# Phase 2 of a fused attention and two-stage MLP kernel: a bank for each product of the last groups, w_out blocks merged in the first half, a fixed order in the second

## The chip, the cores and the metric

The kernel runs on one core of a Trainium2 chip. The metric is the device time of one execution in microseconds; the time before is the median of three runs. A profiled execution of the same kernel gives the rows below.

## The reference

```
attn = softmax(scale * q k^T + slope * bias, causal window of 128) v      # 4 x 8 heads, 576 tokens, 64 wide
x = attn as 2304 tokens x 512
y = ((x w1) * (x w2)) w3 w_out_1          # 512 -> 1024 -> 512
h = max(y w_in, 0)                        # 512 -> 2048
out = (h * h) w_out                       # 2048 -> 512
```

All weights are float64 (the draws of NumPy are not cast), the activations and the output float32.

## The kernel before

Phase 1 (to 458.8 us of the span) makes y, transposed, in DRAM (y_scr). Phase 2 does the last two lines of the reference, and it alone is changed.

Every float32 product is made of three matmuls, since an operand is split into a high part (rounded by a copy, on ACT or DVE) and a low part (the difference, on DVE or POOL): high x high, high x low, low x high (mm3s, L1130 to 1133). A product that reads a high part can start before the low part is there, until its third matmul.

Both halves of phase 2 use Winograd's form of Strassen: a 2 x 2 block product is seven products P1 to P7 and some sums. Sums of inputs are made ahead (combine, L856; comb in add_o, L1275); sums of outputs behind: with U2 = P1 + P6 and U4 = U2 + P5 the blocks are C11 = P1 + P2, C12 = U4 + P3, C21 = U2 + P7 + P4, C22 = U4 + P7, up to signs that lie in the inputs.

*First half (add_r, L1209):* 24 groups (r, j, m) for three blocks j of 768 tokens and eight pairs m of columns of w_in. A product is six matmuls of 384 columns. The results get a relu and go to DRAM (s_scr, L1228). *Second half (add_o, L1243):* nine groups (o, t) of 256 tokens; a product is 24 matmuls of 256 columns over all eight blocks of w_out. Its inputs come back from s_scr (L1253), are squared on ACT (L1261), combined on DVE (L1275), and split into high (L200) and low parts (L203), tiles ww, st or u.

A group (add_group, L1147) has three PSUM banks, tags xa, xb and xc with two buffers each. xa gathers P1, P6, P5, P3, and between them it is copied out: C11 starts as P1 (task c1), C21 as U2 (u2), C22 as U4 (u4); so P6 waits for c1, P5 for u2 and P3 for u4. P7 and P4 gather in xb, P2 in xc; adds on DVE (L1192) finish the blocks. Tasks copy by L200 or L1183 (relu) on ACT and L260 on DVE.

Weights come as float64, two words per element. A block is merged to float32 words by three instructions: ACT scales the high words (L330), DVE shifts the low ones (L339) and ORs both (L345). w_in's blocks and blocks 5 to 7 of w_out are merged in phase 1 and kept in DRAM (add_merge, L870, m_scr); blocks 0 to 4 of w_out are loaded and merged in the last third of the first half (add_words2, L879). Then each block gets four sums (L868), a high and a low copy of the four plain parts (tile u) and of the three sums (tile v).

Every task (products, copies, adds, DMAs) has a rank, dependences, tiles to take and to give back, and a planner (Plan.run) writes all of them out in one order by its own costs; each engine's queue then holds its tasks in that order and runs them one behind the other, SP's DMAs as well. In add_group the order within a group is free but for the dependences, and P4 depends on P7 in all cases. A group called with last (the last of the first half, and (o, 0)) has a second xc bank (tag xd) for P4.

Of the kernel before, what the change touches and what calls it, by code (L numbers as in the profile page):

```python
# [152 lines left out]
def fused_kernel(  # L153
# [56 lines left out]
    NM = NF2 // 2  # L210
    s_scr = [dram.tile([NF2, 128, 2 * TN], F32, name=f"s_scr{j}") for j in range(NJ)]
    m_scr = {(k, m): dram.tile([128, 1024], F32, name=f"m_scr{k}{m}") for k in "ic" for m in range(NM)}
    m_scr.update({("o", m): dram.tile([128, 1024], F32, name=f"m_scro{m}") for m in range(OM, NM)})


    ident = const.tile([128, 128], F32, name="ident")
# [579 lines left out]
    A_AT = {1: "a0", 2: "a1", 3: "b2", 4: "a3", 5: "b0", 6: "b1", 7: "a2"}  # L796
    B_AT = {1: "a0", 2: "a2", 3: "a3", 4: "b2", 5: "b0", 6: "b1", 7: "a1"}
    PO = (1, 2, 6, 7, 5, 3, 4)
    ORDER = ((1, 2, 4, 6, 7, 5, 3), PO)
    lastp = [None]  # L800
    pool = {}
    late = ExitStack()
# [344 lines left out]
    def add_group(g, n, prod, fin, rank, last=False):  # L1147
        z = "".join(str(x) for x in g)
        w = 24 * w_mm(256) if g[0] == "o" else 6 * w_mm(TN)
        for nm, tag in (("xa", "xa"), ("xb", "xb"), ("xc", "xc"), ("C11", "D1"), ("C21", "D2"), ("C22", "D4"), ("C12", "D3")):  # L1150
            hold(nm + z, tag, 1)
        steps = [
            (1, "xa", [], True), (2, "xc", [], True), (6, "xa", ["c1"], False), (7, "xb", [], True),
            (5, "xa", ["u2"], False), (3, "xa", ["u4"], False), (4, "xb", ["c22"], False),
        ]
        if last:
            hold("xd" + z, "xc", 1)
            p4 = (4, "xd", [], True)
            steps = [*steps[:2], steps[3], p4, steps[2], *steps[4:6]] if g[0] == "r" else [*steps[:2], p4, *steps[2:6]]
        for i, (P, nm, dep, first) in enumerate(steps):  # L1160
            deps, gives, fn = prod(P)
            deps = deps + [d + z for d in dep] + {6: [f"P1{z}"], 5: [f"P6{z}"], 3: [f"P5{z}"], 4: [f"P7{z}"]}.get(P, [])
            if P == 1 and lastp[0]:
                deps = deps + lastp
            if P == 1:
                lastp[0] = f"P1{z}"

            def go(e, P=P, nm=nm, first=first, fn=fn, **kw):
                if first and not kw.get("c0"):
                    bank[g, nm] = new("xc" if nm == "xd" else nm, [128, 512])[:, 0:n]  # L1170
                fn(bank[g, nm], first, **kw)

            if g == ("o", 0) and P in (1, 2):
                add(f"Q{P}{z}", rank + i, {"pe": 0.75 * w}, lambda e, go=go: go(e, c0=0, c1=6),
                    [d for d in deps if d[-2:] not in ("o6", "o7")], [nm + z])
                add(f"P{P}{z}", rank + i, {"pe": 0.25 * w}, lambda e, go=go: go(e, c0=6, c1=NM), deps + [f"Q{P}{z}"], [], gives)
            else:
                add(f"P{P}{z}", rank + i, {"pe": w}, go, deps, [nm + z] if first else [], gives)
# [19 lines left out]
        if last:  # L1198
            plus("d21", "21", "xb", ["u2", "P7", "c22"], ["xb"], -20)
            plus("c21", "21", "xd", ["d21", "P4"], ["xd"], -20)  # L1200
        else:
            plus("c21", "21", "xb", ["u2", "P4", "c22"], ["xb"], -20)
        if g[0] == "r":
            add("c12" + z, -20, w_act(n), lambda e: cp(e, "12", "D3", ACTF.Relu), [f"P3{z}"], [f"C12{z}"], [f"xa{z}"])
        else:
            add("c12" + z, -20, w_copy(n, True), lambda e: cp(e, "12", "D3"), [f"P3{z}"], [f"C12{z}"], [f"xa{z}"])
        fin(z)

    def add_r(j, m, rank, last):  # L1209
# [8 lines left out]
        def fin(z):  # L1218
            def relu(e, c):
                x = cs[g, c]  # L1220
                if e == "a":
                    nc.scalar.activation(out=x, in_=x, func=ACTF.Relu)  # L1222
                else:
                    nc.vector.tensor_scalar(out=x, in0=x, scalar1=0.0, scalar2=None, op0=ALU.max)

            def st(c):
                i, h = int(c[0]) - 1, int(c[1]) - 1
                nc.sync.dma_start(out=s_scr[j][m + NM * i, :, TN * h:TN * h + TN], in_=cs.pop((g, c)))  # L1228

            for c in ("11", "12", "21", "22"):  # L1230
                if c != "12":
                    add(f"sq{c}{z}", rank + 16, w_act(TN), lambda e, c=c: relu(e, c), [f"c{c}{z}"])
                add(f"ss{c}{z}", -15, {"dma": w_dma(197)}, lambda e, c=c: st(c), [f"sq{c}{z}" if c != "12" else f"c12{z}"], [], [f"C{c}{z}"])

        add_group(g, TN, prod, fin, rank, last)


    ow = {}
    fa = {}
    FT = {"A11": "fo", "A21": "fo", "A12": "fq", "A22": "fq", "S1": "fq", "S2": "fq"}  # L1240
    A_OF = {1: "A11", 2: "A12", 3: "S2", 4: "A22", 5: "S1", 6: "S2", 7: "A21"}

    def add_o(t, rank, last):  # L1243
        j, t0 = divmod(256 * t, 2 * TN)
# [38 lines left out]
        order = ORDER[t > 0]  # L1283
        chain = {}
        for tag_ in (True, False):
            seq = [P for P in order if (P in (1, 2)) == tag_]
            before = [P for P in ORDER[t > 1] if (P in (1, 2)) == tag_][-1]
            for x, P in enumerate(seq):
                chain[P] = [f"oh{seq[x - 1]}{t}"] if x else [f"oh{before}{t - 1}"] if t else []
        for pos, P in enumerate(order):  # L1290
# [30 lines left out]
            for c in ("11", "12", "21", "22"):  # L1321
                add(f"ss{c}{z}", -15, {"dma": w_dma(131)}, lambda e, c=c: st(c), [f"c{c}{z}"], [], [f"C{c}{z}"])

        add_group(g, 256, prod, fin, rank, t == 0)


    load_order = [("w3", 0), ("wo", 0), ("w3", 1), ("wo", 1), ("wo", 2), ("w3", 2), ("wo", 3)] + [("w3", i) for i in range(3, 8)]
# [145 lines left out]
```

## Time and profile before

| | |
|---|---|
| median of three runs | 826.41 us (826.1 to 827.46) |
| the profiled execution's own time | 828.39 us |
| its span, first to last instruction | 826.6 us |
| mean granted clock of TensorE | 0.998 of full |
| busy: PE, DVE, ACT, POOL | 807.8, 612.3, 467.4, 60.3 us |
| phase 2, first half | 458.8 to 639.6 us |
| phase 2, second half | 639.6 us to the end |

PE is TensorE's matmuls, DVE is VectorE, ACT ScalarE, POOL GpSimd, SP the engine that issues DMAs. Matmuls overlap: each row of one lasts longer than the step to the next, so a busy PE is not PE at its peak, and steps from start to start tell its pace. A row's idle time ends with what released it. Rows with one line number (L200, L203) are those of helpers; their tiles tell them apart.

### The profile page before, as it was taken

To read this page: it belongs to the slowest core of one execution; us is meant where nothing else is said; L and a number is where in the kernel's file an instruction comes from. 1 tells how busy PE (TensorE), PEld (TensorE's weight loads), DVE (VectorE), ACT (ScalarE), POOL (GpSimd) and SP (SyncE) were. 2 spreads that over 40 slices of the span, in tenths; PEclk is the share of its full clock that TensorE was granted. 3 is DMA by queue.
4 is the path that set the end of the run, shared out by engine and by line. 5 is a ranking of instruction groups with operands and counts; after the bars stand their busy time and mean duration, and the time that the engine had idled before them with its cause. 6 is when DMAs were issued, how large, how long until landed. Compare 5 with 4: busy or idle time off the path is not lost.

```text
span 826.6 us, 17260 instructions
## 1 busy us (share of the span) xinstructions
PE 807.8 (98%) x6732; PEld 750.2 (91%) x6732; DVE 612.3 (74%) x1359; ACT 467.4 (57%) x1007; POOL 60.3 (7%) x68
## 2 busy tenths in 40 slices
PE   8899999999999999999999999999999899999998
PEld 7666556699999899999999999999998899999998
DVE  6898888966798997897498565523697887676762
ACT  7898978633333442342244576645688766666531
POOL 1000000000001000210040220000114010000000
PEclk9999999999999999999999999999999999999999
DMA  9989897798623542112231553522894755444200
GB/s 228 288 257 282 272 280 248 273 328 273 213 83 118 192 174 85 63 33 73 63 127 64 182 179 125 193 104 102 288 300 149 210 156 152 133 143 135 87 27 33
DMA packets 96961, 138.75 MB, mean 168 GB/s; under 512 B 10864, under 2 KB 74864, under 8 KB 94832
## 3 DMA queue, kind: packets, MB, share of 16 engines
q1 hardware_dynamic: 96880, 137.65, 53.2%
q8 instruction: 53, 0.87, 0.5%
q14 instruction: 28, 0.23, 0.1%
HBM read 95.81 MB, written 41.81 MB: 167 GB/s over the span
## 4 chain that ended last, share of the span: by engine, by line
PE 89%; DVE 6%; ACT 2%; DMA 1%; issue 1%; POOL 0%; SPq 0%; DVEq 0%; POOLq 0%; ACTq 0%
PE xa L1131 8%; PE xa L1133 8%; PE xa L1132 8%; PE g L659 6%; PE g L195 6%; PE g L196 6%; PE g L197 6%; PE xb L1131 4%; PE xb L1133 4%; PE xb L1132 4%; PE s L467 3%; PE al L1080 3%; PE al L1082 3%; PE al L1081 3%; PE t L503 2%; PE xc L1131 2%
## 5 line engine op out<-in xcount | busy, mean ns | idle before, releaser
L1192 DVE TENSOR_TENSOR D<-xb,D 128x384 f32<-128x384 f32 (+1 forms) x66 | 34.0, 518 | 59.8 <-PE xb L1133 30.8
L196 PE MATMUL g<-gt,wu 128*128 128x288 f32 x256 | 75.7, 296 | 0.0
L195 PE MATMUL g<-gt,wu 128*128 128x288 f32 x256 | 75.6, 295 | 0.0
L197 PE MATMUL g<-gt,wu 128*128 128x288 f32 x256 | 75.4, 295 | 0.0
L200 ACT ACTIVATE D<-xa 128x384 f32<-128x384 f32 (+1 forms) x100 | 45.2, 454 | 40.9 <-PE xa L1133 38.8
L443 ACT ACTIVATE e<-e,st 128x192 f32<-128x192 f32 (+1 forms) x144 | 62.2, 435 | 9.1 <-DVE st L435 8.8
L659 PE MATMUL g<-raw 128*128 128x512 f32 x128 | 62.5, 603 | 0.2
L203 DVE TENSOR_TENSOR ww<-fq,ww 128x1024 fp32r<-128x1024 f32 x34 | 41.6, 1222 | 24.2 <-ACT ww L200 23.8
L1080 PE MATMUL al<-x,wc 128*128 128x288 f32 x192 | 57.5, 299 | 1.1 <-ACT d L200 1.1
L1082 PE MATMUL al<-x,wc 128*128 128x288 f32 x192 | 56.7, 295 | 0.0
L200 ACT ACTIVATE ww<-fq 128x1024 fp32r<-128x1024 f32 x35 | 37.0, 1057 | 34.8 <-PE xa L1133 18.6
L1081 PE MATMUL al<-x,wc 128*128 128x288 f32 x192 | 56.6, 295 | 0.0
L200 ACT ACTIVATE ye<-g 128x288 f32<-128x288 f32 x32 | 13.1, 410 | 73.5 <-PE g L197 68.0
L1222 ACT ACTIVATE D<-D 128x384 f32<-128x384 f32 x72 | 37.2, 521 | 24.3 <-DVE D L1192 24.2
L196 PEld LDWEIGHTS g<-gt,wu 128*128 128x128 f32 x256 | 48.3, 189 | 0.0
L197 PEld LDWEIGHTS g<-gt,wu 128*128 128x128 f32 x256 | 48.2, 188 | 0.0
L195 PEld LDWEIGHTS g<-gt,wu 128*128 128x128 f32 x256 | 48.1, 188 | 0.0
L868 DVE TENSOR_TENSOR st<-st 128x256 f32<-128x256 f32 (+1 forms) x103 | 40.7, 428 | 9.1 <-DMA st<-m_scrc 5.5
L200 ACT ACTIVATE d<-al 128x288 f32<-128x288 f32 x71 | 28.7, 409 | 32.2 <-PE al L1082 23.6
L503 PEld LDWEIGHTS t<-ident,e 128*128 128x128 f32 x208 | 23.7, 140 | 22.6 <-ACT pt L200 9.9
L435 DVE CUSTOM_DVE_ANT_0 e<-s,bw 128x192 f32<-128x192 f32 (+1 forms) x128 | 40.6, 351 | 3.3 <-PE s L467 3.1
L467 PE MATMUL s<-qk 64*64 64x128 f32 (+2 forms) x768 | 38.2, 287 | 4.6 <-issue 1.9
(269 smaller groups left out, 2787.5 us busy)
## 6 DMA issues: line engine op xcount, KB each, us to landing
s_scr<-D SPq DMA_DIRECT2D x96, 192.0 KB, 1.9
u<-in_w2io_dram SPq DMA_DIRECT2D x22, 512.0 KB, 7.5
fo<-s_scr SPq DMA_DIRECT2D x20, 512.0 KB, 4.6
qk<-in_qk_dram SPq DMA_DIRECT2D x32, 288.0 KB, 5.9
st<-m_scrc SPq DMA_DIRECT2D x18, 512.0 KB, 3.8
raw<-in_w3t_dram SPq DMA_DIRECT2D x8, 1024.0 KB, 8.1
raw<-in_w_dram SPq DMA_DIRECT2D x8, 1024.0 KB, 8.3
fq<-s_scr SPq DMA_DIRECT2D x16, 512.0 KB, 4.8
```

The lines of the kernel that those rows point to most:

```text
L195: nc.tensor.matmul(o, wh, xh, start=start, stop=False)
L196: nc.tensor.matmul(o, wh, xl, start=False, stop=False)
L197: nc.tensor.matmul(o, wl, xh, start=False, stop=stop)
L200: nc.scalar.activation(out=o, in_=i, func=ACTF.Copy)
L467: nc.tensor.matmul(HD[2 * m + r]["s"][g][o, c:c + w], t[h, 0, 64 * q:64 * q + 64], t[h, 1, 64 * k:64 * k + w], start=True, stop=True,)
L659: nc.tensor.matmul(gw[fi], wl, wr, start=c == 0, stop=c == 7)
L1080: nc.tensor.matmul(o, wh, xh, start=start and c == 0, stop=False, skip_group_check=True)
L1081: nc.tensor.matmul(o, wh, xl, start=False, stop=False, skip_group_check=True)
L1082: nc.tensor.matmul(o, wl, xh, start=False, stop=c == 1, skip_group_check=True)
L1131: nc.tensor.matmul(o, wh, xh, start=start, stop=False, skip_group_check=True)
L1132: nc.tensor.matmul(o, wh, xl, start=False, stop=False, skip_group_check=True)
L1133: nc.tensor.matmul(o, wl, xh, start=False, stop=stop, skip_group_check=True)
```

## The change

1. A new add_last takes the place of add_group for the last group of each half, (r, 2, 7) and (o, 8). Every product has a bank of its own: P1 and P5 in xa, P6 and P3 in xb, P2 and P4 in xc, P7 in a bank of the older pool g. The products stand in the order 1, 6, 5, 3, 2, 7, 4. Only P1 is copied; u2, u4, c12, c11, d21, c22 and c21 are adds on DVE of a bank and an SBUF block. In (r, 2, 7) C12 then gets its relu by an instruction of its own.
2. Blocks 0 to 4 of w_out are merged by add_merge too, in the first half of phase 2, one after the other in the one free buffer of tag u, behind the last weights of w_in; the words are stored in m_scr and loaded back when add_words2 needs them.
3. In (o, 0) P4 no longer depends on P7. The turns of the second half's products are written out as a list, each depending on the one before, and ORDER has a row for every t.

```diff
-    m_scr.update({("o", m): dram.tile([128, 1024], F32, name=f"m_scro{m}") for m in range(OM, NM)})
+    m_scr.update({("o", m): dram.tile([128, 1024], F32, name=f"m_scro{m}") for m in (*range(OM, NM), *range(OM))})
...
-    ORDER = ((1, 2, 4, 6, 7, 5, 3), PO)
+    ORDER = ((1, 2, 4, 6, 7, 5, 3), *[PO] * (NT // 256 - 2), (1, 6, 5, 3, 2, 7, 4))
...
     def add_group(g, n, prod, fin, rank):
...
-        if last:
+        first_o = g == ("o", 0)
+        if first_o:
             hold("xd" + z, "xc", 1)
-            p4 = (4, "xd", [], True)
-            steps = [*steps[:2], steps[3], p4, steps[2], *steps[4:6]] if g[0] == "r" else [*steps[:2], p4, *steps[2:6]]
+            steps = [*steps[:2], (4, "xd", [], True), *steps[2:6]]
...
-            deps = deps + [d + z for d in dep] + {6: [f"P1{z}"], 5: [f"P6{z}"], 3: [f"P5{z}"], 4: [f"P7{z}"]}.get(P, [])
+            deps = deps + [d + z for d in dep] + {6: [f"P1{z}"], 5: [f"P6{z}"], 3: [f"P5{z}"], 4: [] if nm == "xd" else [f"P7{z}"]}.get(P, [])
...
+    def add_last(g, n, prod, fin, rank):
+        z = "".join(str(x) for x in g)
+        for nm, tag in (("C11", "D1"), ("C21", "D2"), ("C22", "D4"), ("C12", "D3")):
+            hold(nm + z, tag, 1)
+        use = {1: 1, 6: 1, 5: 1, 3: 1, 2: 1, 7: 2, 4: 1}
+        for i, (P, tag) in enumerate(((1, "xa"), (6, "xb"), (5, "xa"), (3, "xb"), (2, "xc"), (7, "g"), (4, "xc"))):
+            deps, gives, fn = prod(P)
+            hold(f"B{P}{z}", tag, use[P])
...
+            def go(e, P=P, tag=tag, fn=fn):
+                bank[g, P] = (ps_g.tile([128, 512], F32, tag="g", name="g") if tag == "g" else new(tag, [128, 512]))[:, 0:n]
+                fn(bank[g, P], True)
+            add(f"P{P}{z}", rank + 0.1 * i, {"pe": 6 * w_mm(TN) if g[0] == "r" else 24 * w_mm(256)}, go, deps, [f"B{P}{z}"], gives)
...
+        add("c1" + z, -30, w_copy(n, True), one, [f"P1{z}"], [f"C11{z}"], [f"B1{z}"])
...
+                nc.vector.tensor_tensor(out=cs[g, o], in0=bank[g, P], in1=cs[g, b], op=ALU.add)
...
+        plus("u2", 6, "11", "21", "D2", ["c1"], -30)
+        plus("u4", 5, "21", "22", "D4", ["u2"], -30)
+        plus("c12", 3, "22", "12", "D3", ["u4"], -20)
+        plus("c11", 2, "11", "11", None, ["c1", "u2"], -20)
+        plus("d21", 7, "21", "21", None, ["u4"], -20)
+        plus("c22", 7, "22", "22", None, ["c12"], -20)
+        plus("c21", 4, "21", "21", None, ["d21"], -20)
+        fin(z)
...
-        add_group(g, TN, prod, fin, rank, last)
+        (add_last if last else add_group)(g, TN, prod, fin, rank)
...
-        add_group(g, 256, prod, fin, rank, t == 0)
+        (add_last if last else add_group)(g, 256, prod, fin, rank)
...
+        if (k, m) == ("o", 0):
+            prev = ["wlbi7"]
         add_merge(k, m, RANK["mg"] + RANK["mgs"] * x, prev)
...
-        prev = [f"{'mb' if m >= OM else 'ld'}o{m}"]
+        prev = [f"mbo{m}"]
+    turn = ["Q1o0", "P1o0", "Q2o0", "P2o0", "P4o0", "P6o0", "P7o0", "P5o0"]
+    for t in range(1, NT // 256):
+        turn += [f"P1o{t}", f"P3o{t - 1}", *([f"P4o{t - 1}"] if t > 1 else []), *(f"P{P}o{t}" for P in ((2, 6, 7, 5) if t < NT // 256 - 1 else (6, 5, 3, 2, 7, 4)))]
+    for x, y in zip(turn, turn[1:]):
+        turns[y] = [x]
     for t in range(NT // 256):
-        add_o(t, r, False)
+        add_o(t, r, t == NT // 256 - 1)
```

(Q1 and Q2 of (o, 0) are the first three quarters of P1 and P2, which need blocks 0 to 5 only.)

DVE's queue at the seam of the two halves, before: the end of group (r, 2, 7) and the inputs of (o, 0). The tiles u and v behind st are low parts of weights, u and ww behind fo and fq low parts of inputs of the second half, D the blocks of a group, fq<-fo and fq<-fq,fo the combinations.

```order
L203 TENSOR_TENSOR u<-st,u 128x1024
L1192 TENSOR_TENSOR D_7584<-xb,D_7584 128x384
L203 TENSOR_TENSOR v_7639<-st,v_7639 128x768
L260 COPY D_7666<-xa 128x384
L1192 TENSOR_TENSOR D_7666<-xb,D_7666 128x384
L1192 TENSOR_TENSOR D_7652<-xb,D_7652 128x384
L1192 TENSOR_TENSOR D_7652<-xc,D_7652 128x384
L203 TENSOR_TENSOR u<-fo,u 128x1024
L203 TENSOR_TENSOR v_7680<-st,v_7680 128x768
L1275 TENSOR_TENSOR fq<-fo 128x1024
L1275 TENSOR_TENSOR fq<-fq,fo 128x1024
L203 TENSOR_TENSOR ww<-fo,ww 128x1024
```

The same place after (L1238 is the add of add_last, L1319 the combinations):

```order
L1238 TENSOR_TENSOR D_7657<-xb,D_7622 128x384
L203 TENSOR_TENSOR u<-st,u 128x1024
L1238 TENSOR_TENSOR D_7669<-xa,D_7657 128x384
L203 TENSOR_TENSOR st<-fo,st 128x1024
L1238 TENSOR_TENSOR D_7622<-xc,D_7622 128x384
L1238 TENSOR_TENSOR D_7689<-xb,D_7669 128x384
L1238 TENSOR_TENSOR D_7669<-g,D_7669 128x384
L1238 TENSOR_TENSOR D_7657<-g,D_7657 128x384
L1238 TENSOR_TENSOR D_7657<-xc,D_7657 128x384
L1319 TENSOR_TENSOR fq<-fo 128x1024
L203 TENSOR_TENSOR u<-fo,u 128x1024
L1319 TENSOR_TENSOR fq<-fq,fo 128x1024
```

The low part of P1's input (st<-fo) is now on DVE, ahead of the group's last five adds; before it was on POOL. The low part of block 7's sums (v<-st) has left this row for POOL. P2's low part (u<-fo) stood ahead of the first combination (fq<-fo) and stands behind it now.

SP's queue in the first half after the change, around the store of block 2 (m_scro) and the load for block 3 (u<-in_w2io_dram, two halves); s_scr<-D are stores of the groups' results. Before, only rows of the kind s_scr<-D stood here.

```order
L1270 DMA s_scr_93<-D_6619 128x384
L849 DMA m_scro_116<-u 128x1024
L1270 DMA s_scr_93<-D_6713 128x384
L1270 DMA s_scr_93<-D_6723 128x384
L1270 DMA s_scr_93<-D_6742 128x384
L1270 DMA s_scr_93<-D_6695 128x384
L843 DMA u<-in_w2io_dram 128x1024 x2
```

The load for block 3 stands behind the last store of group (r, 1, 2) (D_6695); it reuses the buffer that the store of block 2 reads.

ACT's queue after the change, around the scaling of block 3 (L330):

```order
L1264 ACTIVATE D_6762<-D_6762 128x384
L1264 ACTIVATE D_6790<-D_6790 128x384
L200 ACTIVATE D_6828<-xa 128x384
L330 ACTIVATE u<-u 128x1024
L200 ACTIVATE D_6846<-xa 128x384
L200 ACTIVATE D_6855<-xa 128x384
```

The scaling stands between two copies out of bank xa: behind that of U2 of group (r, 1, 4) (D_6828) and ahead of that of U4 (D_6846), for which P3 of the group waits. The other four stand in like places.

## Rows read from the trace of the kernel before

**Rows 1.** The page, busy time, share of the span and instructions of each engine.

```profile
PE 807.8 (98%) x6732; PEld 750.2 (91%) x6732; DVE 612.3 (74%) x1359; ACT 467.4 (57%) x1007; POOL 60.3 (7%) x68
```

**Rows 2.** Table of stretches: length, busy PE, PEld, DVE, ACT, POOL, clock, DMA, GB/s.

```profile
458.76:574.15 115.39, 115.39 (x656) 115.39 (x655) 56.83 (x99) 69.23 (x141) 12.63 (x13) 1.00 0.45 155
574.15:639.58 65.43, 63.85 (x355) 62.19 (x355) 51.60 (x82) 52.56 (x91) 15.39 (x13) 1.00 0.73 236
639.58:661.02 21.44, 19.08 (x145) 18.66 (x145) 18.28 (x18) 15.97 (x19) 0.65 (x1) 0.92 0.73 206
661.02:814.06 153.04, 153.04 (x1298) 153.04 (x1297) 110.26 (x115) 87.69 (x105) 2.96 (x1) 1.00 0.40 114
814.06:823.60 9.54, 8.95 (x74) 8.54 (x72) 0.50 (x2) 0.77 (x2) 0.00 (x0) 1.00 0.09 29
```

**Rows 3.** Timeline of TensorE: start, length, instruction, idle before it and releaser.

```profile
632.38 0.44 PE L1131 MATMUL xa<-yA,v 128*128 128x384 f32 x1 [0.26 <-ACT D L200]
...
636.46 0.44 PE L1131 MATMUL xa<-yA,v 128*128 128x384 f32 x1 [0.63 <-ACT D L200]
...
638.43 0.44 PE L1131 MATMUL xa<-yA,v 128*128 128x384 f32 x1 [0.65 <-DVE D L260]
...
640.28 0.39 PE L1133 MATMUL xa<-u,st 128*128 128x256 f32 x1 [0.29 <-POOL st L203]
...
648.37 0.39 PE L1133 MATMUL xa<-u,ww 128*128 128x256 f32 x1 [2.07 <-DVE ww L203]
...
817.52 0.39 PE L1131 MATMUL xa<-u,ww 128*128 128x256 f32 x1 [0.47 <-ACT D L200]
```

**Rows 4.** Table of stretches, the one behind the wait at 648.37; columns as in rows 2.

```profile
648.37:652.70 4.33, 4.33 (x23) 4.33 (x24) 3.35 (x3) 2.50 (x3) 0.00 (x0) 0.61 0.98 281
```

**Rows 5.** Timeline of DVE around the seam: start, length, instruction.

```profile
629.16 1.76 DVE L203 TENSOR_TENSOR u<-st,u 128x1024 fp32r<-128x1024 f32 x1
630.85 0.55 DVE L1192 TENSOR_TENSOR D<-xc,D 128x384 f32<-128x384 f32 x1
...
642.10 1.21 DVE L1275 TENSOR_TENSOR fq<-fo 128x1024 f32<-128x1024 f32 x1
643.35 1.22 DVE L1275 TENSOR_TENSOR fq<-fq,fo 128x1024 f32<-128x1024 f32 x1
644.49 1.22 DVE L203 TENSOR_TENSOR ww<-fo,ww 128x1024 fp32r<-128x1024 f32 x1
645.63 1.22 DVE L1275 TENSOR_TENSOR fo<-fo 128x1024 f32<-128x1024 f32 x1
```

**Rows 6.** The page, costliest groups: the relu of a block on ACT.

```profile
L1222 ACT ACTIVATE D<-D 128x384 f32<-128x384 f32 x72 | 37.2, 521 | 24.3 <-DVE D L1192 24.2
```

**Rows 7.** Timeline of DVE, the last instruction of the program's last chain.

```profile
823.52 0.42 DVE L1192 TENSOR_TENSOR D<-xb,D 128x256 f32<-128x256 f32 x1 [5.60 <-PE xb L1133]
```

**Rows 8.** Timeline of DVE, the shift and the OR of a block's merge.

```profile
607.41 0.68 DVE L339 TENSOR_SCALAR st<-st 128x1024 uint32<-128x1024 uint32 x1
...
608.94 1.21 DVE L345 SCALAR_TENSOR_TENSOR st<-st 128x1024 uint32<-128x1024 uint32 x1
```

**Rows 9.** Table of stretches of 20 us; columns as in rows 2.

```profile
500.00:520.00 20.00, 20.00 (x115) 20.00 (x114) 11.12 (x21) 12.96 (x30) 0.73 (x1) 1.00 0.35 118
540.00:560.00 20.00, 20.00 (x115) 20.00 (x114) 4.46 (x8) 9.06 (x19) 0.00 (x0) 1.00 0.33 118
600.00:620.00 20.00, 20.00 (x115) 20.00 (x115) 19.74 (x34) 17.26 (x30) 3.22 (x3) 1.00 0.96 297
```

**Rows 10.** Timeline of POOL near the seam: start, length, instruction, idle before.

```profile
627.60 3.92 POOL L868 TENSOR_TENSOR st<-st 128x256 f32<-128x256 f32 x3 [1.92 <-DMA st<-m_scro]
```

**Rows 11.** A late load: SP's issue, ACT's scaling; and the issues of 603 to 607 us.

```profile
581.63 0.85 SPq L843 DMA_DIRECT2D st<-in_w2io_dram  x2
...
589.68 1.18 ACT L330 ACTIVATE st<-st 128x1024 f32<-128x1024 f32 x1 [0.87 <-DMA st<-in_w2io_dram]
...
st<-in_w2io_dram SPq DMA_DIRECT2D x2, 512.0 KB, 5.7
```

More of the change, by code (lines that the diff above doesn't have):

```diff
@@ L1145, in p_o, with add_group @@
             mm3s(o, a[:, 0, 128 * c:128 * c + 128], a[:, 1, 128 * c:128 * c + 128], bh, bl, start and c == 0, c == NM - 1)
[L1147 removed]
+    def add_group(g, n, prod, fin, rank):
         z = "".join(str(x) for x in g)
@@ L1171, in go @@
                 fn(bank[g, nm], first, **kw)
-            if g == ("o", 0) and P in (1, 2):
+            if first_o and P in (1, 2):
                 add(f"Q{P}{z}", rank + i, {"pe": 0.75 * w}, lambda e, go=go: go(e, c0=0, c1=6),
-                    [d for d in deps if d[-2:] not in ("o6", "o7")], [nm + z])
+                    [d for d in deps if d[-2:] not in ("o6", "o7")] + turns.get(f"Q{P}{z}", []), [nm + z])
                 add(f"P{P}{z}", rank + i, {"pe": 0.25 * w}, lambda e, go=go: go(e, c0=6, c1=NM), deps + [f"Q{P}{z}"], [], gives)
             else:
-                add(f"P{P}{z}", rank + i, {"pe": w}, go, deps, [nm + z] if first else [], gives)
+                add(f"P{P}{z}", rank + i, {"pe": w}, go, deps + turns.get(f"P{P}{z}", []), [nm + z] if first else [], gives)
         def cp(e, c, tag, func=None):
@@ L1197, in add_group @@
         plus("c11", "11", "xc", ["c1", "P2"], ["xc"], -20)
-        if last:
+        if first_o:
             plus("d21", "21", "xb", ["u2", "P7", "c22"], ["xb"], -20)
@@ L1206, in add_group, with one, plus, fn @@
             add("c12" + z, -20, w_copy(n, True), lambda e: cp(e, "12", "D3"), [f"P3{z}"], [f"C12{z}"], [f"xa{z}"])
+        fin(z)
[7 more added lines that the diff above has]
+            hold(f"B{P}{z}", tag, use[P])
+            if P == 1:
+                deps = deps + lastp
+                lastp[0] = f"P1{z}"
+            deps = deps + turns.get(f"P{P}{z}", [])
+            def go(e, P=P, tag=tag, fn=fn):
+                bank[g, P] = (ps_g.tile([128, 512], F32, tag="g", name="g") if tag == "g" else new(tag, [128, 512]))[:, 0:n]
+                fn(bank[g, P], True)
+            add(f"P{P}{z}", rank + 0.1 * i, {"pe": 6 * w_mm(TN) if g[0] == "r" else 24 * w_mm(256)}, go, deps, [f"B{P}{z}"], gives)
+        def one(e):
+            t = cs[g, "11"] = new("D1", [128, TN])[:, 0:n]
+            copy(e, t, bank[g, 1])
+        add("c1" + z, -30, w_copy(n, True), one, [f"P1{z}"], [f"C11{z}"], [f"B1{z}"])
+        def plus(nm, P, b, o, tag, deps, rank):
+            def fn(e):
+                if tag:
+                    cs[g, o] = new(tag, [128, TN])[:, 0:n]
+                nc.vector.tensor_tensor(out=cs[g, o], in0=bank[g, P], in1=cs[g, b], op=ALU.add)
+            add(nm + z, rank, w_tt(n, "d"), fn, [f"P{P}{z}"] + [d + z for d in deps], [f"C{o}{z}"] if tag else [], [f"B{P}{z}"])
+        plus("u2", 6, "11", "21", "D2", ["c1"], -30)
[5 more added lines that the diff above has]
+        plus("c21", 4, "21", "21", None, ["d21"], -20)
         fin(z)
@@ L1230, in fin @@
             for c in ("11", "12", "21", "22"):
-                if c != "12":
+                if c != "12" or last:
                     add(f"sq{c}{z}", rank + 16, w_act(TN), lambda e, c=c: relu(e, c), [f"c{c}{z}"])
-                add(f"ss{c}{z}", -15, {"dma": w_dma(197)}, lambda e, c=c: st(c), [f"sq{c}{z}" if c != "12" else f"c12{z}"], [], [f"C{c}{z}"])
-        add_group(g, TN, prod, fin, rank, last)
+                add(f"ss{c}{z}", -15, {"dma": w_dma(197)}, lambda e, c=c: st(c), [f"sq{c}{z}" if c != "12" or last else f"c12{z}"], [], [f"C{c}{z}"])
+        (add_last if last else add_group)(g, TN, prod, fin, rank)
     ow = {}
@@ L1241, in fused_kernel @@
     A_OF = {1: "A11", 2: "A12", 3: "S2", 4: "A22", 5: "S1", 6: "S2", 7: "A21"}
+    turns = {}
     def add_o(t, rank, last):
@@ L1282, in add_o @@
         src = {1: f"fsA11{t}", 6: f"fc1{t}", 2: f"fsA12{t}", 7: f"fc2{t}", 5: f"fc0{t}", 3: f"fc3{t}", 4: f"fsA22{t}"}
-        order = ORDER[t > 0]
+        order = ORDER[t]
         chain = {}
@@ L1286, in add_o @@
             seq = [P for P in order if (P in (1, 2)) == tag_]
-            before = [P for P in ORDER[t > 1] if (P in (1, 2)) == tag_][-1]
+            before = [P for P in ORDER[t - 1] if (P in (1, 2)) == tag_][-1]
             for x, P in enumerate(seq):
```

## The prediction, made before the changed kernel ran

> **What bounds the kernel now.** I read the page's busy times first: TensorE is busy 98% of the span [rows 1], so only what TensorE waits, or runs slowly, can be won. Next, the table of stretches, cut where phase 2 changes its work [rows 2]. In the first stretch TensorE does 109 products of six matmuls, 654 in all (two more reach in from the phase before), in 115.39 us: 0.1764 us each, with no wait. At that pace the 354 matmuls of the second stretch (the last 59 products of the first half) need 62.46 us and take 65.43: **2.97 lost**. In the fourth stretch 54 products of 24 matmuls, 1,296 in all, take 153.04 us: 0.1181 each, no wait. So the third stretch (six products, 144 matmuls) needs 17.00 us and takes 21.44: **4.44 lost**. In the last stretch P5 to P3 of the last group should start 24 x 0.1181 = 2.83 us apart; P3 starts at 817.52 [rows 3] instead of 816.90, and its restart adds about 0.1: **0.75 lost**. All of phase 2 has 8.16 us that a gapless order would not have.
>
> Then the timeline of TensorE, to see what each wait was for [rows 3]. Its idle figure understates the loss, since a matmul's row lasts longer than its step (0.34 against 0.18, 0.28 against 0.12): add 0.16 to each. Three waits for copies out of bank xa (P3 of group (2,6), P5 and P3 of (2,7)) cost 0.42, 0.79 and 0.81, with 0.1 for each restart 2.3 of the 2.97; some 0.65 is left in small pieces. At 640.28 the first product of the second half waits for a low part made on POOL: 0.45. At 648.37 P6 of group (o,0) waits 2.07 for its low part on DVE: 2.23. And behind that wait the granted clock is 0.61 on average over 4.33 us [rows 4], that is, mostly the lower of its two levels: 23 matmuls that need 2.72 us take 4.34, 1.6 more. Last, 817.52 waits for a copy: 0.63.
>
> **The change, part by part.** *Own banks in the last group of each half.* P6, P5 and P3 no longer add onto P1's bank, so TensorE waits for no copy there. That removes the waits of 0.79 and 0.81 at (2,7), with restarts 1.8, and the 0.75 in (o,8). What it adds: u2, u4 and c12 become adds on DVE, about 0.55 each [rows 5], and one relu on ACT, 0.52 [rows 6]. At (o,8) nothing waits for these but the end: there the last chain is one add of a bank and a store, as now [rows 7], so the tail costs what it did. At (2,7) five adds in a row stand on DVE between the low part of P1(o,0) and the combination S1; that is priced below.
>
> *The w_out blocks 0 to 4 merged earlier.* Per block two loads, a scaling on ACT (1.18 us), a shift and an OR on DVE (0.7 and 1.2) [rows 8] move from the stretch 580 to 612 to some 495 to 570. DVE had 19.74 of 20 us busy at 600 to 620, but 11.1 and 4.5 of 20 in the two quieter stretches [rows 9]; 9.5 us of DVE work and 5.8 of ACT fit there. The DMA share was 0.96 in the late stretch, and 0.33 to 0.35 in the others; five stores and five loads back of 0.5 MB each are added, and 5 MB of loads are moved, so the late stretch gets lighter by half of what it loaded. Weights are then ready earlier, DVE is not behind at the seam, P3 of (2,6) no longer waits (0.52 with its restart) and POOL no longer makes the first low part (0.55). Of the small pieces, 0.65, I take 0.2 as left (bounds 0 and 0.65).
>
> *P4 of (o,0) before P6, fixed turns.* P4's wait for P7 was needless with a bank of its own. It now gives TensorE 2.83 us while DVE makes the low part for P6. From the fourth stretch on the order is that of before but for the last group, where there was no wait to win: zero, since no instruction is added there.
>
> *The seam after the change.* Let T be the issue of Q1(o,0). DVE's queue then holds, behind the last add of (2,7): S1, the low part of P2, S2, the low part of P4, the combination for P7, one small add, the low part of P6. The last add ends about T+0.65 (its matmul ends 0.16 after T, then 0.5). By the steps of rows 5, S1 takes 1.25 and each further instruction 1.14: P2's low part is done at T+3.0, P4's at T+5.3, P6's at T+8.0. TensorE has Q1 and P1 to do first, 2.83, and its first two matmuls of Q2 need no low part, 0.24; so Q2 waits 0 to 0.1 and restarts in 0.1. P4 is due at T+5.7 plus 0.24 and P6 at T+8.5: both ready. The doubtful point is the POOL instruction (low part of block 7, 768 wide), which now runs beside this DVE row. DVE's 1024-wide difference took 1.76 us beside POOL work against 1.22 alone [rows 5, 10]; an add with a bank as input did not stretch there (0.55). If two such instructions stretch by 0.54, Q2 waits 1.2 and P4 0.6 of it again at most. Bounds 0.1 and 1.3; I take **0.5**, nearer the plain steps, as POOL should be done before the low part of P2 starts. The Trainium skill (SBUF — State Buffer, Who interferes with whom) says that a DVE instruction with two SBUF inputs contends with a GpSimd instruction that reads SBUF, and that one with at most one does not: both rows agree, and by it the wait would be nearer to 1.3, the time 820.1.
>
> *The new wait.* The scaling and the shift stand in ACT's and DVE's queues and wait for their load; behind them stand the copies and adds that TensorE needs. For the fourth load (block 3) TensorE's order has eight products, 8.5 us, between the product that releases the store in front of the load on SP and the copy in front of the scaling; an add, a relu [rows 5, 6] and the issue take 1.5 to 2, so 6.5 to 7 us are left for the load (a later one if the block's store before it lands late). Measured: the median half lands in 5.7 us in one window, and the second half is issued 0.4 later; the slowest case went from issue at 581.63 to 589.68, 8.05 us, in a busy stretch [rows 11]. ACT's copy has about half a product of slack, 0.5 us. Bounds for all five: 0, and 5 x (8.05 - 6.5 - 0.5) = 5.3. The first half moves a third as much as that stretch, so I take **0.4**. The Trainium skill (DMA: Bandwidth & Descriptors, Anatomy of one DMA) fits about 2.0 us plus the bytes at 436 GB/s, though for another issuing path: an estimate of 4.4 us for the megabyte, which no row here reaches; by it this term would be zero and the time 818.9.
>
> **Sum.** 8.16 - 0.5 - 0.4 - 0.2 = 7.06 us. The profiled execution took 828.39 (span 826.6): 821.3. The median of the runs is 826.41, 2.0 below it; the same gain gives **819.3**. By its bounds this case alone runs from 818.3 to 820.8.
>
> **The rivals.** *Loads late in the first half.* For: single-file ACT and DVE, and each load waits for the store before it. Against: DMA at a third. With two to five loads as late as the slowest, 2 to 5 us come back: 821.3 to 824.2.
>
> *The seam still waits.* For: DVE has some fifteen instructions in a row there and POOL runs beside them. If Q2 waits as long as P6 did, 2.1 instead of 0.5, and the clock falls behind it as in rows 4, that is 1.6 + 1.6: 822.5. Against: seven more low parts or weights are ready than before.
>
> *Slower.* The wait at the five scalings is long enough that TensorE stops as at 648.37. From a landing of about 8.8 us on, the five cost more than the 8.7 that it takes to turn the gain into a loss of over 0.2%; if each costs what 648.37 did with its slow clock, 3.85, the time is 819.3 + 18.9 = 838. Against: no load in the trace is that late, even at three times the traffic.
>
> *The words are not made earlier in effect.* DVE does the same instructions, and if the waits for weights and low parts just move to the next product of the seam, all but the 0.75 of the last group and the 1.8 of (2,7) returns: 824 to 825. Against: the order shows every word ahead of its use by several DVE instructions.
>
> **Chances.** Forecast 0.74, late loads 0.12, seam 0.07, no earlier words 0.03, slower 0.04. Range 818.2 to 823.2: it holds the forecast with its bounds, the seam and most of the late loads. A measurement of this kernel tells 0.2%, 1.65 us, from no change; so faster than 824.8: 0.92; same: 0.04; slower: 0.04.
>
> **What would show it.** Right: in the profile after, no wait of TensorE at P5 and P3 of (2,7) nor at P3 of (o,8); at the seam at most one wait of about half a microsecond, at Q2, and the clock at 1.00 throughout; the first product of the second half about 2.4 us earlier (2.97 - 0.2 - 0.4), the first of group (o,1) about 6.3 earlier (4.44 - 0.5 more), and the same add and store at the end. Wrong: ACT waiting for the load in front of the scaling with TensorE idle behind it, or a wait over 2 us at the seam with a granted clock under 1.

## The result, and the profile after

| | before | after |
|---|---|---|
| median of the runs (4 each, side by side) | 826.82 us | 819.83 us (819.4 to 821.09) |
| ratio, 95% interval | | 0.9918 (0.9901 to 0.9935) |
| profiled execution, its span | 828.39, 826.6 us | 819.97, 818.1 us |
| phase 2, first half | 180.82 | 178.14 |
| first product of the second half to the first of (o,1) | 21.44 | 17.39 |
| from there to the end of the span | 165.57 | 165.17 |

The time fell by 7.0 us, 0.8%; 819.3 had been forecast. Phase 2 went from 367.83 to 360.70 us, that is by 7.13, against 7.06 forecast. The other 1.37 us between the two spans lie in phase 1, which the change does not touch (it ended at 458.77 and 457.40).

The page's busy times after, as [rows 1], and the table of stretches, cut at the start of phase 2, at the first product of the second half and at the first of (o,1) (columns as in [rows 2]):

```profile
PE 803.4 (98%) x6732; PEld 747.6 (91%) x6732; DVE 613.3 (75%) x1361; ACT 466.7 (57%) x1006; POOL 57.5 (7%) x69
```

```profile
457.40:635.54 178.14, 178.14 (x1010) 177.77 (x1009) 109.24 (x182) 121.18 (x230) 26.19 (x27) 1.00 0.65 215
635.54:652.93 17.39, 17.28 (x146) 17.08 (x145) 14.17 (x15) 12.72 (x16) 0.05 (x1) 1.00 0.82 234
652.93:818.10 165.17, 162.00 (x1370) 161.58 (x1368) 115.39 (x121) 91.33 (x110) 2.50 (x1) 1.00 0.39 112
```

TensorE is busy 4.4 us less with the same matmuls, 2.9 of it in these three stretches (360.30 before, 357.42 after). Of the 2.9, 1.8 lie at the seam (19.08 before, 17.28 after), where no matmul ran at the slow clock; 1.1 lie in the first half, where a part of each wait had counted as busy. DVE has as much to do as before. 1,008 matmuls at 0.1764 need 177.8 us: 0.33 is left in the first half, of 3.0. The seam needs 17.00: 0.39 is left of 4.44. The clock is 1.00 in all three, where [rows 4] had 0.61. None of the six waits of [rows 3] is there any more. The one stop at the seam shows in TensorE's timeline only as steps of 0.38 and 0.22 instead of 0.12, at the third matmul of Q2, which needs the low part; 0.37 is lost in all:

```profile
638.54 0.28 PE L1132 MATMUL xc<-u 128*128 128x256 f32 x1
638.92 0.39 PE L1133 MATMUL xc<-u 128*128 128x256 f32 x1
639.14 0.28 PE L1131 MATMUL xc<-u 128*128 128x256 f32 x1
```

DVE's timeline there (start, length, instruction), the counterpart of [rows 5]:

```profile
634.92 1.02 DVE L1238 TENSOR_TENSOR D<-g,D 128x384 f32<-128x384 f32 x2
636.04 0.56 DVE L1238 TENSOR_TENSOR D<-xc,D 128x384 f32<-128x384 f32 x1
636.52 1.22 DVE L1319 TENSOR_TENSOR fq<-fo 128x1024 f32<-128x1024 f32 x1
637.65 1.22 DVE L203 TENSOR_TENSOR u<-fo,u 128x1024 fp32r<-128x1024 f32 x1
...
639.92 1.22 DVE L203 TENSOR_TENSOR ww<-fo,ww 128x1024 fp32r<-128x1024 f32 x1
...
642.53 1.22 DVE L203 TENSOR_TENSOR ww<-fq,ww 128x1024 fp32r<-128x1024 f32 x1
```

With T = 635.54, the low parts of P2, P4 and P6 end at T + 3.33, 5.60 and 8.21 (forecast 3.0, 5.3, 8.0): S1 begins at T + 0.98, behind the last add, instead of 0.65. P4 and P6 have room; Q2 waits for the first.

The program's end is as in [rows 7], an add behind the last matmul:

```profile
814.97 0.42 DVE L1238 TENSOR_TENSOR D<-xc,D 128x256 f32<-128x256 f32 x1 [2.06 <-PE xc L1133]
```

One loss was not foreseen: 0.35 us at P7 and P5 of (o,1). Two things come together there. A load of inputs lands late: ACT waits 1.32 for it before it can square it, and DVE, whose queue is next, waits 2.11 for the square. Then one combination takes DVE 3.32 us, beside an instruction of POOL. From 652.7 to 668 DVE has no gap. (It is not so from 636.5 on, as one expectation below has it: DVE also waits 0.94 at 649.39.) The rows of ACT, DVE and POOL:

```profile
651.63 1.06 ACT L1305 ACTIVATE fq<-fq 128x1024 f32<-128x1024 f32 x1 [1.32 <-DMA fq<-s_scr]
```

```profile
652.72 1.23 DVE L1319 TENSOR_TENSOR fq<-fo,fq 128x1024 f32<-128x1024 f32 x1 [2.11 <-ACT fq L1305]
653.98 3.32 DVE L1319 TENSOR_TENSOR fq<-fq,fo 128x1024 f32<-128x1024 f32 x1
```

```profile
633.54 2.05 POOL L203 TENSOR_TENSOR v<-st,v 128x768 fp32r<-128x768 f32 x1 [11.98 <-ACT v L200]
653.71 2.50 POOL L203 TENSOR_TENSOR st<-fq,st 128x1024 fp32r<-128x1024 f32 x1 [18.12 <-ACT st L200]
```

### The profile page after: what moved, and what is told of

Same layout as the page of the kernel before. It is cut to its first block, busy times and chain, and to the rows that moved or that the text cites. A ratio compares the mean times of both kernels' runs of the same rounds, so it can differ in the third digit from the quotient of the medians.

```text
span 818.1 us, 17284 instructions
## 1 busy us (share of the span) xinstructions
PE 803.4 (98%) x6732; PEld 747.6 (91%) x6732; DVE 613.3 (75%) x1361; ACT 466.7 (57%) x1006; POOL 57.5 (7%) x69
## 5 line engine op out<-in xcount | busy, mean ns | idle before, releaser
L1192 DVE TENSOR_TENSOR D<-xb,D 128x384 f32<-128x384 f32 (+1 forms) x62 | 32.2, 520 | 37.8 <-PE xb L1133 18.0
```

## The experiments

The change has three parts: the **banks**, the early **merge**, and **P4** ahead of P6. They were run in all eight combinations, with two small liberties: banks and merge keeps the fixed turns of the groups behind (o,0), and merge and P4 keeps the banks of their own in (o,8). The theory on record adds their worth up; its rival says that each has its worth only where the others have made room on DVE. This table has the time from the first product of phase 2 to the first of (o,1), read from each kernel's timeline (in brackets a second execution of the same kernel), and the medians. The times in the first column are of single executions, and two of one kernel differ by up to 2.69 us; the medians and ratios are of 4 to 10 runs each.

| kernel | first half + seam, us | median, us | ratio to before |
|---|---|---|---|
| before | 202.26 | 826.2 to 826.8 in three comparisons, 825.3 in one | |
| banks alone | 199.47 (199.26) | 824.24 | 0.9984 (0.9968 to 0.9999) |
| merge alone | 203.16 | 827.58 | 1.0018 (1.0003 to 1.0033) |
| P4 alone | 197.93 | 823.49 | 0.9952 (0.9932 to 0.9971) |
| banks and P4 | 197.93 (200.62) | 823.46 | 0.9960 (0.9945 to 0.9975) |
| banks and merge | 197.66 | 822.57 | 0.9955 (0.9936 to 0.9975) |
| merge and P4 | 200.49 | 825.29 | 0.9994 (0.9974 to 1.0014) |
| all three (after) | 195.53 (195.53) | 819.83, again 820.22 | 0.9918 (0.9901 to 0.9935), again 0.9927 (0.9907 to 0.9946) |

**Banks alone** (before, with this in both places):

```diff
-        add_group(g, TN, prod, fin, rank, last)
+        (add_last if last else add_group)(g, TN, prod, fin, rank)
```

> The kernel before with add_last for the last group of each half, and nothing else of the change. Theory A (the parts add up): the waits of 0.79 and 0.81 at (2,7) with their restarts go (1.8) and the 0.75 of (o,8); the seam keeps its 4.4: 826.8 - 2.55 = 824.3, first half 179.0 us, seam (first product of the second half to the first of (o,1)) 21.4. Theory B (the banks pay only where DVE has its other work behind it): the low parts of the weights of blocks 6 and 7 are still made at the seam, and behind them the low part that the first product needs; what TensorE wins at (2,7) it waits again ahead of the second half. Then only the 0.75 stays: 826.1, first half 179.0, seam 23.2 or more, with a wait of over 1.5 us at the first product of the second half.

First half 178.10, seam 21.37. All but 0.3 of the first half's loss is gone, also the 0.52 of P3 of (2,6), which had been put down to the merge: the planner now lays the products of (2,6) and (2,7) in another order. (The small pieces are gone as well, but that is not the banks' doing; see P4 alone.) But Q1, the first product of the second half, waits for its low part, which stands behind the weights' low parts on DVE. Theory B holds at the seam, A in the first half. TensorE's timeline and the seam's row of the table of stretches, first execution:

```profile
638.32 0.48 PE L1133 MATMUL xa<-u,st 128*128 128x256 f32 x1 [2.58 <-DVE st L203]
```

```profile
635.32:656.69 21.37, 18.79 (x145) 18.59 (x145) 18.76 (x20) 16.30 (x21) 1.28 (x1) 0.92 0.78 224
```

The same kernel once more (one run, 824.46 us):

> The kernel with the banks alone, once more. Its first trace shows 2.58 us of idle TensorE at Q1 and a granted clock at the lower level for 3.5 us behind it. If the fall belongs to that wait, it is there again and the seam takes 21.4; if it depends on the run, the seam may take 19.8, as long as the wait allows at full clock.

```profile
639.37 0.38 PE L1133 MATMUL xa<-u,st 128*128 128x256 f32 x1 [2.57 <-DVE st L203]
...
646.31 0.38 PE L1133 MATMUL xa<-u,ww 128*128 128x256 f32 x1 [0.93 <-DVE ww L203]
```

```profile
636.37:657.57 21.20, 17.70 (x146) 17.28 (x146) 18.68 (x20) 15.67 (x21) 1.27 (x1) 1.00 0.81 226
```

The same wait, and no slow clock behind it. Yet the seam is as long: at full clock P6 comes to its low part before DVE does, and waits 0.93 there. So here the slow clock cost next to nothing; DVE's row sets the length.

**Merge alone** (before, with this and the two lines of the change on prev):

```diff
-    m_scr.update({("o", m): dram.tile([128, 1024], F32, name=f"m_scro{m}") for m in range(OM, NM)})
+    m_scr.update({("o", m): dram.tile([128, 1024], F32, name=f"m_scro{m}") for m in (*range(OM, NM), *range(OM))})
```

> The kernel before with blocks 0 to 4 of w_out merged early, and nothing else of the change (the order of the products at the seam comes from the planner again, and it lays three products of (2,7) between those of (o,0)). Theory A: P3 of (2,6) waits no more (0.52), POOL no longer makes the first low part (0.55), the small pieces shrink from 0.45 to 0.26 (as the changed kernel shows): 826.8 - 1.3 = 825.5, with P6 of (o,0) still waiting some 2 us and the clock falling behind it. Theory B (the late words were the cause of the wait at P6 too): DVE comes to the low part of P6 some 2 us earlier, the wait and the slow stretch go, 826.8 - 1.3 - 3.8 = 821.7.

Neither: it is slower. P6 stops twice, for the high part on ACT and then for the low part, 5.18 us together, with the clock at 0.50 behind it. In the first half no wait is left here either: P3 of (2,6), whose group the planner has reordered too, does not wait. TensorE's timeline, then DVE's:

```profile
643.35 0.58 PE L1131 MATMUL xa<-u,ww 128*128 128x256 f32 x1 [3.66 <-ACT ww L200]
...
645.67 0.58 PE L1133 MATMUL xa<-u,ww 128*128 128x256 f32 x1 [1.52 <-DVE ww L203]
```

```profile
639.78 0.42 DVE L1196 TENSOR_TENSOR D<-xc,D 128x256 f32<-128x256 f32 x1 [1.41 <-issue]
640.12 0.95 DVE L203 TENSOR_TENSOR v<-st,v 128x768 fp32r<-128x768 f32 x1
640.99 1.22 DVE L1323 TENSOR_TENSOR fq<-fq,fo 128x1024 f32<-128x1024 f32 x1
```

With the words early, the planner lays P5 and P3 of (2,7) between the products of (o,0) to hide the copies of the shared bank. That puts the last adds of (2,7), a low part and the small add C11 of (o,0), which itself waits for P2, ahead of the combination (640.99) that P6 needs.

**P4 alone** (before, with this, where first_o is true for (o,0), and the list of turns):

```diff
-            deps = deps + [d + z for d in dep] + {6: [f"P1{z}"], 5: [f"P6{z}"], 3: [f"P5{z}"], 4: [f"P7{z}"]}.get(P, [])
+            deps = deps + [d + z for d in dep] + {6: [f"P1{z}"], 5: [f"P6{z}"], 3: [f"P5{z}"], 4: [] if first_o else [f"P7{z}"]}.get(P, [])
```

> The kernel before with P4 of (o,0) freed from P7 and the fixed turns of the second half (P4 ahead of P6; the last group in its old order), and nothing else of the change. Theory A: DVE's queue at the seam is that of before, where the low part of P4 ends at 645.71 and that of P6 at 648.31; P4 is due at 645.90 and P6 2.83 later, so neither waits and the clock stays at 1.00: 826.8 - 2.23 - 1.6 = 823.0, seam 17.6, first half as before (180.8). Theory B (DVE is the bound of the seam, whatever TensorE's order): the time between the first product of the second half and the first of (o,1) stays over 19.5, a wait of about 2 us shows at P7 or at P1 of (o,1): 825 or more.

Theory A: seam 17.57, with the 0.45 at Q1 as its only wait, clock 1.00. The first half takes 180.36 with its three waits, not 180.8. Up to P3 of (2,6) all engines have the very order of the kernel before there; yet 0.45 us of the small pieces is gone. So these belonged to the profiled execution of the kernel before, not to the kernel. There ACT's first scaling of a w_out block waited 0.87 for its load [rows 11], and TensorE lost its small pieces just behind it; here it waited 0.18:

```profile
589.30 1.16 ACT L330 ACTIVATE st<-st 128x1024 f32<-128x1024 f32 x1 [0.18 <-DMA st<-in_w2io_dram]
```

**Banks and P4, no merge** (after, with the words of blocks 0 to 4 made late again):

```diff
-    m_scr.update({("o", m): dram.tile([128, 1024], F32, name=f"m_scro{m}") for m in (*range(OM, NM), *range(OM))})
+    m_scr.update({("o", m): dram.tile([128, 1024], F32, name=f"m_scro{m}") for m in range(OM, NM)})
```

> The changed kernel with blocks 0 to 4 of w_out merged late, as before; banks, P4 and turns as changed. Theory A (the parts add up): 819.8 + 1.3 = 821.1. Theory B (the banks pay only where DVE has its other work behind it): the low part for the first product of the second half stands behind the low parts of the weights and the last adds of (2,7), TensorE waits over 1.5 us there, and what the banks gained at (2,7) is lost with it: 823.0 to 824.0, seam 19 or more. As in the run with the banks alone, a granted clock under 1 may follow such a wait.

Theory B: Q1 waits 2.56. In the first execution the clock stayed at 1.00 behind it, seam 19.88. This execution also lost 0.72 behind (o,1), which the table does not hold: ACT waited 1.57 there for a load of inputs, and the copy that P5 of (o,1) needs stood behind it. In the second execution (one run, 828.48 us) the clock did not stay:

> The changed kernel without the early merge, once more. Its first trace shows 2.56 us of idle TensorE at Q1 and the full clock behind it, seam 19.9. If the clock's answer belongs to the wait's length, then this kernel and the one with the banks alone should show the same one; if it depends on the run, this one may show the slow stretch now: seam 21.4.

```profile
643.29 0.39 PE L1133 MATMUL xa<-u,st 128*128 128x256 f32 x1 [2.57 <-DVE st L203]
```

```profile
640.29:661.64 21.35, 18.78 (x145) 18.58 (x145) 17.84 (x19) 15.50 (x20) 1.91 (x2) 0.92 0.80 224
```

Here the slow stretch does cost, 1.47 us. This execution also shows the rival of the late load, in the place that the change empties: ACT's scaling waited 1.97 for a load of w_out, and behind it TensorE 0.96 for a copy (rows of ACT and of TensorE):

```profile
609.98 1.17 ACT L330 ACTIVATE st<-st 128x1024 f32<-128x1024 f32 x1 [1.97 <-DMA st<-in_w2io_dram]
```

```profile
611.57 0.45 PE L1131 MATMUL xa<-yA,v 128*128 128x384 f32 x1 [0.96 <-ACT D L200]
```

**Banks and merge, P6 ahead of P4** (after, with the old turn and P4 behind P7):

```diff
-    turn = ["Q1o0", "P1o0", "Q2o0", "P2o0", "P4o0", "P6o0", "P7o0", "P5o0"]
+    turn = ["Q1o0", "P1o0", "Q2o0", "P2o0", "P6o0", "P7o0", "P4o0", "P5o0"]
```

> The changed kernel with the order P6, P7, P4, P5 in (o,0) as before, P4 behind P7; banks, early merge and the fixed turns of the other groups as changed. Theory A (P4's place is what covers DVE's row): DVE's queue at the seam is unchanged, and in the changed kernel the low part of P6 ended at 643.75, while P6 would now be due 2.83 earlier, its third matmul at 641.9. So P6 waits 1.85 us and a restart: seam 17.39 + 1.95 = 19.3, or some 1.6 more if the granted clock falls behind the wait; 821.8 to 823.4. Theory B (with the words merged early DVE has its lead anyway): a wait under 0.6 us at P6, seam under 18.0, 820.4 or less.

Theory A, seam 19.53. The clock did not fall:

```profile
643.33 0.39 PE L1133 MATMUL xa<-u,ww 128*128 128x256 f32 x1 [1.73 <-DVE ww L203]
```

**Merge and P4, shared banks in (2,7)** (after, with add_group there, and the second xc bank for P4 as before):

```diff
-        (add_last if last else add_group)(g, TN, prod, fin, rank)
+        add_group(g, TN, prod, fin, rank)
```

> The changed kernel with the last group of the first half in shared banks again, as before (the planner then lays P5, P3 of (2,7) between the first products of (o,0)); the rest as changed. Theory A (the parts add up): P5 and P3 of (2,7) wait for copies or are covered by products of (o,0); 0 to 1.8 us are lost: 819.8 to 821.6. Theory B (the end of (2,7) sets when DVE can begin with the second half's inputs): as in the run with the merge alone, the first combination starts only behind adds that wait for late products of (2,7), and the small sum C11 of (o,0) stands in front of the next ones; P4's low part ends about 3.4 us after it is due there. A wait of 3 to 3.5 us at P4, with or without a slow clock (1.6) behind it: 823.0 to 824.8.

Theory B: as with the merge alone, the second combination comes late, and P4 stops twice, with a slow clock behind:

```profile
642.88 0.39 PE L1131 MATMUL xc<-u,ww 128*128 128x256 f32 x1 [1.61 <-ACT ww L200]
...
644.98 0.39 PE L1133 MATMUL xc<-u,ww 128*128 128x256 f32 x1 [1.60 <-DVE ww L203]
```

**What is left at (o,1) and at the seam.** Three versions of the kernel after, and itself again. First, the low parts of the second half's inputs only on DVE (the four combinations likewise):

```diff
-            add(f"ol{P}{t}", rank + pos + early, w_tt(1024), lo, [f"oh{P}{t}"], [], F(k))
+            add(f"ol{P}{t}", rank + pos + early, w_tt(1024, "D"), lo, [f"oh{P}{t}"], [], F(k))
```

> The changed kernel with one difference in effect: the low part for P2 of (o,1) is made on DVE instead of POOL. In the changed kernel a combination on DVE took 3.32 us beside that POOL instruction (1.22 elsewhere), DVE was busy without a gap from 636.5 to 668, and TensorE lost 0.35 us at P7 and P5 of (o,1). Theory A (the two engines block each other there, and this is what TensorE waits for): the combination takes 1.22, the low part 1.22 more, DVE is 0.96 us earlier at P7 of (o,1), the loss there goes; from the first of (o,1) to the end 161.65 instead of 162.00 us (last matmul), time 819.5. Theory B (DVE is full with or without POOL): one more instruction of 1.22 on DVE, the loss at P7 and P5 stays or grows to over 0.6: 819.8 to 820.5.

The combination took 1.23, the loss at (o,1) was gone: phase 2 to its last matmul 357.16 us, against 357.53. The median was 820.28 (ratio 0.9932, 0.9906 to 0.9957).

```profile
653.28 1.23 DVE L1319 TENSOR_TENSOR fq<-fq,fo 128x1024 f32<-128x1024 f32 x1
```

That is what theory A said, but the kernel after itself did as well the second time:

> The changed kernel itself, once more, on the chip of the run above it. If the lengths read from a trace belong to the kernel: phase 2 to its last matmul 357.5 within 0.2 us, seam 17.4, the wait of 0.37 at Q2 and the 0.35 at P7 and P5 of (o,1) again. If they are a matter of the run, they differ by as much as the times of the runs do (2 us).

First half 178.15, seam 17.38 with 0.38 at Q2 again, but no loss at (o,1), phase 2 357.18. The block by POOL was there (rows of DVE and POOL):

```profile
653.70 3.32 DVE L1319 TENSOR_TENSOR fq<-fq,fo 128x1024 f32<-128x1024 f32 x1
```

```profile
653.43 2.51 POOL L203 TENSOR_TENSOR st<-fq,st 128x1024 fp32r<-128x1024 f32 x1 [17.29 <-ACT st L200]
```

The block is real; counted from Q1, though, this row began 0.84 earlier than in the first trace (17.60 against 18.44 us), since a load of inputs had landed earlier (ACT waited 0.50 for it to square it, 1.32 in the first). So the block alone costs TensorE nothing; with the later load it may have. Whether taking POOL away saves the 0.35 then is open: the run without POOL began its combination at 18.10, between the two.

Next, P2's low part ahead of the first combination, and then P4's ahead of the second:

```diff
-        add(f"fc0{t}", rank, w_tt(1024), lambda e: comb(0, e), [f"fsA21{t}", f"fsA22{t}", "q2"], F("S1"), F("A21", "A22"))
+        add(f"fc0{t}", rank, w_tt(1024, "D"), lambda e: comb(0, e), [f"fsA21{t}", f"fsA22{t}", "q2"] + (["ol20"] if t == 0 else []), F("S1"), F("A21", "A22"))
-        add(f"fc1{t}", rank, w_tt(1024), lambda e: comb(1, e), [f"fsA11{t}", f"fc0{t}"], F("S2"), F("S1", "A11"))
+        add(f"fc1{t}", rank, w_tt(1024, "D"), lambda e: comb(1, e), [f"fsA11{t}", f"fc0{t}"] + (["ol40"] if t == 0 else []), F("S2"), F("S1", "A11"))
```

(The second pair is in the later version only.)

> As the run with that low part on DVE, and besides the low part for P2 of (o,0) is made ahead of the first combination. Theory A: the wait at Q2 (0.37) goes, DVE's later instructions stand where they were (the two just change places), and P7 of (o,1) still does not wait: seam 17.02, all of phase 2 357.53 - 0.72 = 356.8 us to its last matmul, time 819.1. Theory B (DVE bounds the stretch up to 668): what TensorE wins at Q2 it waits again at P4, P6 or in (o,1), so phase 2 stays at 357.2 or more: 819.5.

> As the run before it with the low part of P2 ahead (there Q2's wait of 0.37 went, but P4 of (o,0) waited 0.24), and besides P4's low part is made ahead of the second combination. Theory A (DVE's row at the seam has room, only its order was wrong): P2's low part at Q1 + 2.5, P4's 2.3 later, due at Q1 + 5.9; P6's low part stays at about Q1 + 8.7, due at Q1 + 8.74; no wait over 0.1 at the seam, seam 17.1, phase 2 to its last matmul 356.9 to 357.0 us. Theory B (the row is full): the 0.24 moves on to P6 or into (o,1), phase 2 stays at 357.2.

With the first, Q2's 0.37 went and 0.24 came at P4: theory B, seam 17.36. With both, 0.09 is left at P6: theory A, seam 17.18, phase 2 356.95 us. The medians were 818.73 (ratio 0.9918, 0.9890 to 0.9945) and 820.00 (0.9923, 0.9910 to 0.9936); beside 819.83 and 820.22 no version beats the change by what a measurement tells.

## Why the prediction was right, and where not

The whole came out within 0.1 us (7.06 forecast, 7.13 measured), and that is in part luck. The first half gave 2.68 instead of 2.37, the seam 4.05 instead of 3.94, and the rest behind (o,1) 0.40 instead of 0.75.

*First half, 2.97 less 0.6: held (0.33 left),* with two terms put down to the wrong cause. P3 of (2,6), 0.52, was put down to the merge, but the banks alone remove it, and so does the merge alone; in both, the planner had put the products in another order. Of the small pieces, 0.45 of 0.65 were the one execution's (P4 alone, above).

*The loads, 0.4: no wait at all.* In none of the eight executions with the early merge did ACT stand idle in front of any of the five scalings. What these executions lose, and the six without do not, is 0.13 at P5 of (1,5): the copy in front of it begins on ACT after 0.21 of idle time, behind a relu and not behind a scaling. Why it is late is open. The issue and the scaling of block 3 (SP, ACT):

```profile
542.80 0.84 SPq L843 DMA_DIRECT2D u<-in_w2io_dram  x2
```

```profile
550.12 1.13 ACT L330 ACTIVATE u<-u 128x1024 f32<-128x1024 f32 x1
```

ACT came to the scaling 7.3 us after the issue, straight from a copy, and did not wait; 6.5 to 7 had been reckoned. The margin was thin all the same. For block 2 DVE's shift did wait for the load, and began 0.31 before ACT came to its scaling; DVE had the time to spare, and TensorE lost nothing there:

```profile
535.00 0.70 DVE L339 TENSOR_SCALAR u<-u 128x1024 uint32<-128x1024 uint32 x1 [0.63 <-DMA u<-in_w2io_dram]
```

```profile
535.31 1.15 ACT L330 ACTIVATE u<-u 128x1024 f32<-128x1024 f32 x1
```

*The seam, 4.44 less 0.5: held (0.39 left),* at Q2, as forecast. The reason for the doubt fell, though: POOL's low part (633.54 to 635.59) ran beside adds that read a bank, which stayed at 0.55, and not beside the long row. The 0.33 by which P2's low part was late came from two adds out of bank g in front of the last add, which the sum did not have. The Trainium skill (SBUF — State Buffer, Who interferes with whom) has the two kinds apart in the same way, and calls the ports that they share an exclusive lock, in which the order of issue decides who waits. The trace agrees: the combination that began 0.27 behind POOL took 3.32, some 1.1 of it behind POOL's end at 656.21.

*The parts as separate terms: not borne out.* Alone, P4 was worth 4.33 us up to (o,1), the banks 2.79, the merge -0.90; with the two others in place 2.13, 4.96 and 2.40. These are differences of single executions, and each of the three values alone counts what only that execution of the kernel before had: the 0.45 of small pieces, and the slow clock. That they sum to 6.22, close to the 6.73 of the whole, says little. The ratios of the runs say it more safely: alone, P4 is worth 0.48% of the time, the banks 0.16% and the merge -0.18%, together 0.46%, where the whole change is worth 0.82% and, the second time, 0.73%. With the two others in place, the banks are worth at least 0.67% and the merge at least 0.33%, both clear of what they are worth alone. So what the banks and the merge are worth depends on the other parts; for P4 (0.28 to 0.37% with the others) the runs do not settle it. The step "weights are then ready earlier, DVE is not behind at the seam" named the cause and priced it at POOL's 0.55; with the banks in, late weights cost a wait of 2.56 to 2.58 at Q1. This is the term that the prediction sized too small for a part by itself; in its sum for the whole change it did no harm, since there the weights are early.

*The slow clock, 1.6: a term of the profiled execution, not of the kernel.* The sum counted it as if it came every time. In three series of 27, 24 and 11 runs of the kernel before, 20 of the 62 kept a mean clock of 1.00, and their medians lie 1.6 to 2.6 us below those of the others. In the series that has both kernels at 1.00, the change is still worth 6.0 us (825.59, three runs, against 819.56, four).

*The last group, 0.75: right.* From (o,1) to the last matmul 162.46 us became 161.65 in the second trace after, as in eight other executions with own banks in (o,8); in the first trace, 0.35 was given back at (o,1).

*The rivals.* With the whole change none of them came: no scaling waited for a load, no wait at the seam was longer than half a microsecond, the clock stayed at 1.00 in both traces, and the kernel is not slower. The seam's wait with the slow clock is what the merge without the banks shows, and there the time was 827.58 and, with P4, 825.29: the words are early and DVE's row at the seam is late even so.

*One bound.* The upper end of the case's own bounds, 820.8, is not the sum of the bounds named there: the seam and the small pieces give 820.55, and with 5.3 us for the loads it would be 825.45. The stated range, up to 823.2, covers the one and not the other.

## What to carry to other kernels

Here a table of waits gave the gain of the whole change well, and that of its parts badly: when a wait goes, the same late producer can be met at the next product. So ask of each part alone what the late engine's queue still has in front of what is needed next. Where a planner orders the work, an edit that only makes something earlier may let it choose an order that is worse on the chip, as with the merge alone. Before a small loss is explained, a second trace of the same kernel, or one in which that stretch is unchanged, can tell whether it belongs to the kernel: the 0.45 of small pieces and the 0.35 at (o,1) did not come a second time.

## What the runs showed of the hardware

TensorE's clock did not give one answer to one wait. Idle for 2.58 and 2.57 us at the same product of the same kernel, it went to the lower level in one execution and stayed at the higher in the other; in the kernel without the merge it was the same, with 2.57 (it fell) and 2.56 (it stayed). After 1.73 us it stayed; after 2.07 in the kernel before it fell [rows 4], and after the two stops of 1.61 and 1.60 of merge and P4 as well (0.60 over the 4.2 us behind them). What decides it these runs do not tell. And its price depends on what is late next: 1.47 us in one kernel, 0.17 in the other, where TensorE would have waited anyway.

A low part or a combination of DVE that began while POOL was at work on one waited for it. A combination on DVE took 3.32 beside a low part on POOL, and in the kernel without the merge a low part on DVE took 3.43 and 3.44 (its two executions) beside a combination on POOL; elsewhere in these traces either takes DVE 1.2. Each time the instruction on POOL had begun first.
